# Two interleaved mixer and MLP layers on one core: finer groups at the hand-over to the first MLP, a new plan of priorities, and a store cut in halves

## The chip, the cores and the metric

The kernel runs on one core of one Trainium2 chip. The metric is device time in microseconds of one execution. The kernel before takes 249.48 us (median of 8 runs, 248.67 to 251.76).

A core has five engines that run their own instruction streams and meet at semaphores: TensorE (PE) multiplies matrices out of SBUF into PSUM; ScalarE (ACT) and VectorE (DVE) both can move PSUM to SBUF; GpSimd (POOL) does small things here; SyncE (SP) issues nearly all DMAs.

## The reference, cut to what matters

```
x = q                                            # (1, 2048, 512) bf16
x = x + layernorm(x) * y                         # mixer A
x = x + gelu(layernorm(layernorm(x)) @ w1 + b1) @ w2 + b2   # MLP B, F = 1376
x = x + layernorm(x) * y                         # A again, same y
x = x + gelu(layernorm(layernorm(x)) @ w1 + b1) @ w2 + b2   # B again
```

Here `y = irfft(rfft(kv) * rfft(ssm_k)) + kv * ssm_D`, and `kv` is the 4-tap causal filter of `k` with `shift_k`, times `v`. It doesn't depend on `x`, so it is computed once. The convolution along 2048 positions, 512 channels, is long; the kernel does it with matrix products in place of an FFT.

## The kernel before, in words

**Data.** The 2048 positions are 16 slices of 128 rows, 512 channels wide. Slice `s` holds positions `16 * p + s` on partition `p`. All SBUF lives in one big array `ar`, cut by hand into regions (`R_X` the running activation, `R_YT` the result `y`, `R_XT` and `R_HT` two buffers each for the transposed input and the hidden layer of the MLP); small floats are in `sm`, and PSUM is `ps`, eight banks.

**The mixer part** runs first and has these stages, each a run of matmuls into a PSUM tile of two banks, followed by an eviction to bf16 in SBUF by ACT or DVE (helper `evac`, L512: L515 is ACT's form, L516 DVE's):

- `ht` (L566 to 579): the filter `ssm_k`, loaded as 4 blocks of 128 channels, is transposed on PE (L573, 16 transposes per block).
- `h1` and `h2` (L608 to 615): two transform stages of the filter, PE lines L590 and L603. When all of `h2` is in `R_H`, 16 DMAs of 256 KB (L620; issued through the helper at L499) copy it to `R_HS` with the two halves of the partitions swapped.
- `fir0` to `fir3` (L623 to 672): the 4-tap filter of `k` for four groups of 128 channels. Groups 0 and 1 go through PE (L633 transposes, L645 products, L652 times `v`); groups 2 and 3 are eight DVE operations each in `shift_dve` (through the helper `tt`, L510). These form three products with taps into three shared temporaries, then add, multiply and add in turn.
- `x1_0` to `x1_3` (first transform of `kv`, L590), then for each half of the channels (`PARTS`: 64 groups of 4 channels each): `x2` (`products`: PE L691, an eviction, then a DVE product with both `R_H` and `R_HS`, L510), `i1` (first inverse stage, PE L715) and `i2` (second inverse stage, `inverse2`, PE L771). `inverse2` makes 4 slices of `y` at a time for one half of the channels: 8 matmuls of 256 columns and one eviction of 1024 columns.

**The MLP part** goes block by block over slices: in layer 0 in blocks of 2, 2, 2, 2, 4, 4 slices (`BLOCKS0`), in layer 1 of 4, 4, 4, 4. A block takes these steps: statistics on DVE (L799, L801) and the power -0.5 on POOL (L805, L807); the normalization on DVE (L814), times `y`, plus `x` (L510); statistics again; the second normalization; four 128 by 128 transposes per slice, on PE with an eviction for slices 0 to 3 of layer 0 (L858) and by DMA on SP's queue for the others (L850); `m1`, 11 groups of 4 matmuls, as wide as 128 times the block's slices (L871), each followed by a GELU on ACT (L876); `m2`, per slice 11 matmuls of 512 columns (L890) and one DVE addition to `x` (L894). In layer 1 finished slices are stored two at a time, 256 KB per DMA.

**The order of work** isn't written down by hand. Every operation is recorded with a cost in ns and its reads and writes; `Prog.schedule` then plays a list scheduler: the engine that can start earliest takes the ready operation of highest priority. The priority is the length of the path behind it plus a bias per stage from the table `BIAS`; `SHY` holds DVE back from evictions of a stage by so many ns; `LAT` is the assumed delay from one engine to another. What comes out is a fixed order for each engine and a choice of engine for every eviction; the costs have no other effect. DMAs keep their program order on SP's queue. `Pool` limits how many PSUM tiles of a kind may be open (four of two banks for the mixer part; two banks for transposes, three for `m1`, three for `m2`). The planner also emits the waits: an operation waits on its own engine too where it reads or overwrites what an earlier one there wrote or read (PE and SP excepted).

Of the kernel before, what the change touches and what calls it, by code (L numbers as in the profile page):

```python
# [44 lines left out]
class Prog:  # L45
# [5 lines left out]
    LAT = 130.0  # L51
    BIAS = {'fir0': 83800, 'fir1': -43400, 'fir2': 54600, 'fir3': -219300, 'h1': 39000, 'h2': 18300, 'ht': 155000, 'i1_0': -114900, 'i1_64': 24300, 'i2_0': -179500, 'i2_64': 54600, 'm1': 74700, 'm2': -45000, 'q0': 3500, 'q1': -4700, 'q2': 145200, 'q3': -6300, 'q5': -57000, 'q6': -80400, 'q7': -74600, 'x1_0': -53700, 'x1_1': 64300, 'x1_2': -7500, 'x1_3': 21300, 'x2_0': 210400, 'x2_64': 68700, 'z0': 9300, 'z1': -23300, 'z2': -64900, 'z3': 38400, 'z5': -30700, 'z6': -33300, 'z7': -12500}
    SHY = {'fir0': 1000, 'fir1': 0, 'h1': 150, 'h2': 0, 'ht': 3000, 'i1_0': 0, 'i1_64': 0, 'i2_0': 150, 'i2_64': 600, 'x1_0': 770, 'x1_1': 300, 'x1_2': 150, 'x1_3': 1000, 'x2_0': 600, 'x2_64': 0, 'z0': 600, 'z1': 600}
# [127 lines left out]
    def schedule(self):  # L181
# [29 lines left out]
        while done < n:  # L211
# [58 lines left out]
            for si in o.succ:  # L270
                q = ops[si]
                lat = self.LAT
                if not o.dma and len(q.engs) == 1 and q.engs[0] == o.eng:
                    lat = 0.0 if o.eng == PE or q.preds[o.i] == "psum" else 90.0
                q.ready = max(q.ready, o.end + lat)
                q.npred -= 1
                if q.npred == 0:
                    for x in q.engs:
                        ready[x].append(q)
# [147 lines left out]
AR = 105088  # L427
PE_CH = (0, 1)
LOADS = ("k", "v", 0, 1, 2, 3, 4, 5, 6, 7)
PARTS = ((0, 64), (64, 64))  # L430
BLOCKS0, BLOCKS1 = (2, 2, 2, 2, 4, 4), (4, 4, 4, 4)
NSPLIT = 4


def bass_interleave_layers__ssm_conv_h3__mixer_channel_mlp__prompt_kernel(
# [52 lines left out]
    R_SR, R_D = R_2, R_2 + 2048  # L488
    R_XT = R_S2
# [30 lines left out]
    E1 = {ACT: 1040.0, DVE: 1220.0}  # L520
# [40 lines left out]


# [4 lines left out]
    for b in range(4):  # L567
# [3 lines left out]
        def f(e, src=src, tl=tl):  # L571
            for a in range(16):
                r = e.transpose(QB(tl, 0, 128, a * 128, [1, 128]), src[a], IDN)  # L573
            return r
        P.op(PE, f, 16 * 80.0, reads=src + [IDN], tile=tl)
        evac(BOTH, A(0, 128, R_HP + b * 2048, [4, 16], [64, 32], [1, 4]),
             lambda tl=tl: QB(tl, 0, 128, 0, [128, 16], [4, 32], [1, 4]), {ACT: 1880.0, DVE: 1225.0}, tl)
# [18 lines left out]
    def stage2(G, ks, n):  # L596
# [8 lines left out]
        P.op(PE, f, len(ks) * 53.0, reads=[x for y in ins for x in y[1:]], tile=tl)  # L605
# [19 lines left out]
    def shift_pe(i):  # L625
# [5 lines left out]
        def f(e, src=src, tl=tl):  # L631
            for a in range(16):
                r = e.transpose(QB(tl, 0, 128, a * 128, [1, 128]), src[a], IDN)  # L633
            return r
        P.op(PE, f, 16 * 60.0, reads=src + [IDN], tile=tl)
        evac(BOTH, A(0, 128, R_KT[i] + 2, [130, 16], [1, 128]),
             lambda tl=tl: QB(tl, 0, 128, 0, [128, 16], [1, 128]), {ACT: 1880.0, DVE: 1225.0}, tl)
        for a8 in range(2):
# [8 lines left out]
            P.op(PE, f, 32 * 62.0, reads=[x for y in ins for x in y[2:]], tile=tl)  # L647
# [5 lines left out]
            P.op(DVE, g, 1200.0, reads=[v], writes=[o], tile=tl)  # L653

    def shift_dve(i):

        c = DV_CH[i]
        tm = [A(0, 128, R_TMP + 2048 * q, [128, 16], [1, 128]) for q in range(3)]

        def tap(j, o):  # L660
            tt(o, A(0, 128, R_K + (3 - j) * 512 + 128 * c, [512, 16], [1, 128]),
               A(0, 128, R_SJ + 512 * i + 128 * j, [0, 16], [1, 128]), ALU.mult, 1210.0,
               more=halo if j else ())
        for j in range(3):
            tap(3 - j, tm[j])
        tt(tm[1], tm[0], tm[1], ALU.add, 1210.0)
        tap(0, tm[0])
        tt(tm[2], tm[1], tm[2], ALU.add, 1210.0)
        tt(tm[1], tm[2], tm[0], ALU.add, 1210.0)
        tt(A(0, 128, R_KV + 2048 * c, [64, 32], [4, 16], [1, 4]),  # L670
           A(0, 128, R_TMP + 2048, [4, 32], [128, 16], [1, 4]),
           A(0, 128, R_V + 128 * c, [4, 32], [512, 16], [1, 4]), ALU.mult, 1220.0)
# [7 lines left out]
    def products(d0, n):  # L680
# [3 lines left out]
        for k0 in range(0, 128, nk):  # L684
# [4 lines left out]
            def f(e, ins=ins, tl=tl):  # L689
                for i, w, m in ins:  # L690
                    r = e.matmul(Q(tl, 0, 128, i * pitch, [1, n]), w, m, start=True, stop=True)  # L691
                return r
            P.op(PE, f, nk * 53.0, reads=[x for y in ins for x in y[1:]], tile=tl)
# [4 lines left out]
                 {ACT: 200 + .82 * w, DVE: 80 + 1.11 * w}, tl)  # L698
            x = A(0, 128, xo, [0, 2], [4 * nk, n // 4], [1, 4 * nk])
            h = A(0, 128, R_H + 128 * d0 + 4 * k0, [R_HS - R_H, 2], [512, n // 4], [1, 4 * nk])  # L700
            tt(h, x, h, ALU.mult, 80 + 1.11 * w)
# [19 lines left out]
    for c in range(4):  # L721
# [3 lines left out]
        else:  # L725
            shift_dve(DV_CH.index(c))
# [29 lines left out]
    def inverse2(d0, n):  # L756
# [3 lines left out]
        for a0 in range(0, 16, 2 * nb):  # L760
            tl = Tile(dconv)
            ins = []
            for al in range(2 * nb):
# [10 lines left out]
            t = 2 * nb * w  # L774
# [159 lines left out]
```

## Time and profile before

| what | value |
|---|---|
| time, median of 8 runs | 249.48 us |
| time of the profiled execution | 249.46 us |
| its span, first to last instruction | 247.7 us |
| mean granted TensorE clock | 0.992 |
| busy: PE, DVE, ACT, POOL | 227.5, 175.6, 136.4, 29.7 us |
| first matmul (transposes of `ssm_k`) | 5.05 us |
| first matmul of `inverse2` | 80.21 us |
| first matmul of the MLP | 89.75 us |
| last PE instruction of the span ends | 244.36 us |

How to read it: the span is 1.76 us shorter than the run's time, and this remainder lies outside what the engines' instructions show. A row of the groups gives the busy time and the mean duration of one instruction; back to back instructions overlap a little, so the pitch (the time of a run of them divided by their number) is shorter than this mean, above all on PE. In the timeline and in the chain, instructions of one line that follow each other are merged, with their count behind the x.

### The profile page before, as it was taken

What the parts mean: (1) busy time and instruction counts of PE and PEld (TensorE: products, weight loads), DVE (VectorE), ACT (ScalarE), POOL (GpSimd) and SP (SyncE); (2) the same over time, 40 slices, a digit from 0 to 9 for tenths busy, and PEclk for the clock granted to TensorE, in tenths of its full rate; (3) what the DMA queues carried; (4) which work ended last, traced back from release to release, by engine and by line L of the source; (5) the groups of instructions that cost most, each with busy time, mean ns of one, the idle gap of its engine ahead of it and who ended that gap; (6) DMA issues with size and microseconds to landing.
All of it is one profiled execution on the core that took longest, in us unless ns stands there. A gap on an engine that the chain in (4) does not pass through costs nothing.

```text
span 247.7 us, 5306 instructions
## 1 busy us (share of the span) xinstructions
PE 227.5 (92%) x2248; PEld 145.0 (59%) x2248; DVE 175.6 (71%) x358; ACT 136.4 (55%) x189; POOL 29.7 (12%) x58
## 2 busy tenths in 40 slices
PE   1988889787699979999999999999999999999994
PEld 1977779576699847775644444444444444444441
DVE  0798999989999888908999996378894732202233
ACT  2377798899998877753506517318228353072000
POOL 2320000000102042110111103005011010000000
PEclk9999999999999979999999999999999999999999
DMA  6999915999994000120130402200407123011112
GB/s 241 371 407 409 396 24 122 216 216 223 369 381 134 0 0 11 34 42 3 22 64 3 85 0 43 42 3 3 85 0 90 42 42 85 3 42 42 42 42 85
DMA packets 25480, 27.64 MB, mean 112 GB/s; under 512 B 17553, under 2 KB 19568, under 8 KB 25328
## 3 DMA queue, kind: packets, MB, share of 16 engines
q1 hardware_dynamic: 25310, 27.21, 37.9%
q8 instruction: 17, 0.28, 0.5%
q10 hardware_dynamic: 146, 0.10, 0.2%
q14 instruction: 7, 0.06, 0.1%
HBM read 17.34 MB, written 2.10 MB: 78 GB/s over the span
## 4 chain that ended last, share of the span: by engine, by line
PE 75%; ACT 7%; SPq 6%; DMA 5%; DVE 4%; issue 1%; DVEq 0%
PE ps L871 32%; PE ps L890 30%; SPq L499 6%; ACT ar L515 6%; PE ps L715 6%; DMA ar<-ar 3%; PE ps L590 2%; DVE ar L510 2%; PE ps L573 2%; DMA ar<-in_A_ssm_k_dram 2%; PE ps L645 2%; DVE ar L516 1%; DVE ar L894 1%; DVE ar L652 0%; ACT ar L537 0%
## 5 line engine op out<-in xcount | busy, mean ns | idle before, releaser
L876 ACT ACTIVATE ar<-ps,sm 128x512 bf16<-128x512 f32 (+3 forms) x110 | 63.5, 601 | 73.9 <-PE ps L871 52.9
L871 PE MATMUL ps<-ar 128*128 128x512 bf16 (+3 forms) x440 | 79.8, 342 | 1.1 <-ACT ar L515 1.1
L515 ACT ACTIVATE ar<-ps 128x1024 bf16<-128x1024 f32 (+2 forms) x76 | 70.7, 1038 | 16.0 <-PE ps L590 13.3
L890 PE MATMUL ps<-ar 128*128 128x512 bf16 (+1 forms) x352 | 78.1, 379 | 0.0
L871 PEld LDWEIGHTS ps<-ar 128*128 128x128 bf16 (+1 forms) x440 | 44.4, 102 | 35.5 <-ACT ar L515 1.2
L510 DVE TENSOR_TENSOR ar<-ar 128x512 bf16<-128x512 bf16 (+2 forms) x104 | 61.0, 643 | 0.9 <-ACT ar L515 0.7
L890 PEld LDWEIGHTS ps<-ar 128*128 128x128 bf16 (+1 forms) x352 | 34.3, 98 | 40.7
L894 DVE TENSOR_TENSOR ar<-ar,ps 128x512 bf16<-128x512 bf16 x32 | 21.1, 682 | 51.0 <-PE ps L890 51.0
L799 DVE BATCH_NORM_STATS2 sm<-ar 128x6 f32<-128x512 bf16 (+1 forms) x68 | 41.0, 646 | 0.0
L814 DVE TENSOR_SCALAR ar<-ar,sm 128x512 bf16<-128x512 bf16 x64 | 22.5, 405 | 7.2 <-POOL sm L807 5.4
L590 PE MATMUL ps<-ar 128*64 128x128 bf16 x512 | 17.8, 221 | 3.9 <-DVE ar L510 1.5
L516 DVE CAST ar<-ps 128x1024 bf16<-128x1024 f32 x17 | 20.1, 1219 | 1.1 <-PE ps L590 0.7
L807 POOL TENSOR_TENSOR sm<-sm 128x4 f32<-128x4 f32 (+1 forms) x20 | 18.6, 931 | 1.7
L590 PEld LDWEIGHTS ps<-ar 128*64 128x64 bf16 x512 | 14.9, 110 | 6.4 <-DVE ar L510 1.7
L805 POOL TENSOR_SCALAR sm<-sm 128x4 f32<-128x4 f32 (+1 forms) x20 | 4.3, 217 | 108.0 <-DVE sm L801 107.9
L715 PE MATMUL ps<-ar 128*128 128x128 bf16 x256 | 14.9, 220 | 1.7 <-DVE ar L510 1.4
L715 PEld LDWEIGHTS ps<-ar 128*128 128x128 bf16 x256 | 14.5, 114 | 1.9 <-DVE ar L510 1.5
L516 DVE COPY ar<-ps 128x2048 bf16<-128x2048 bf16 x5 | 6.1, 1226 | 8.0 <-PE ps L573 7.7
L691 PE MATMUL ps<-ar 128*128 128x64 bf16 x256 | 9.6, 194 | 2.0 <-ACT ar L515 1.5
L573 PE MATMUL ps<-ar 128*128 128x128 bf16 x64 | 5.8, 264 | 5.1 <-DMA ar<-in_A_ssm_k_dram 5.1
L691 PEld LDWEIGHTS ps<-ar 128*128 128x128 bf16 x256 | 8.2, 98 | 3.2 <-ACT ar L515 2.2
L603 PE MATMUL ps<-ar 128*128 128x128 bf16 x128 | 8.4, 220 | 1.8 <-ACT ar L515 0.9
(24 smaller groups left out, 70.7 us busy)
## 6 DMA issues: line engine op xcount, KB each, us to landing
ar<-tab_s SPq DMA_DIRECT2D x8, 512.0 KB, 16.2
ar<-ar SPq DMA_DIRECT2D x16, 256.0 KB, 6.6
ar<-in_A_ssm_k_dram SPq DMA_DIRECT2D x4, 512.0 KB, 5.5
ar<-in_A_k_dram SPq DMA_DIRECT2D x4, 512.0 KB, 9.5
ar<-in_A_v_dram SPq DMA_DIRECT2D x4, 512.0 KB, 13.5
ar<-in_A_q_dram SPq DMA_DIRECT2D x4, 512.0 KB, 12.7
out_dram<-ar SPq DMA_DIRECT2D x8, 256.0 KB, 2.0
ar<-in_B_w_dram SPq DMA_DIRECT2D x1, 1376.0 KB, 11.6
```

What stands on the lines that cost most here:

```text
L510: return P.op(eng, lambda e: e.tensor_tensor(o, a, b, op), dur, reads=[a, b] + list(more), writes=[o])
L515: return e.activation(dst, src(), AF.Copy)
L516: return e.tensor_copy(dst, src())
L590: r = e.matmul(Q(tl, 64 * ri, 64, i * 128, [1, 128]), w, m, start=True, stop=True)
L715: r = e.matmul(Q(tl, 0, 128, i * 128, [1, 128]), w, m, start=q == 0, stop=q == 1)
L799: P.op(DVE, lambda e, sj=sj, x=x: e.bn_stats(sj, x), 80.0 + 1.18 * w, reads=[x], writes=[sj], gate=gate)
L807: P.op(POOL, lambda e: e.tensor_tensor(r, v, hf, ALU.pow), 1020.0, reads=[v, hf], writes=[r])
L814: P.op(DVE, lambda e: e.tensor_scalar(o, x, m, r, ALU.subtract, ALU.mult), 405.0, reads=[x, m, r], writes=[o])
L871: r = e.matmul(Q(tl, 0, rows, 0, [1, w]), a, m, start=dk == 0, stop=dk == 3)
L876: P.op(ACT, lambda e, dst=dst, tl=tl, rows=rows, bias=bias, w=w: e.activation(dst, Q(tl, 0, rows, 0, [1, w]), AF.Gelu_apprx_tanh, bias=bia ...
L890: r = e.matmul(Q(tl, 0, 128, 0, [1, 512]), ins[fc][0], ins[fc][1], start=fc == 0, stop=fc == 10)
L894: P.op(DVE, lambda e, x=x, tl=tl: e.tensor_tensor(x, x, Q(tl, 0, 128, 0, [1, 512]), ALU.add), 690.0, reads=[x], writes=[x], tile=tl)
```

## The change

- **Second inverse stage.** `inverse2` makes slices 0 and 1, then 2 and 3, then 4 to 7, 8 to 11 and 12 to 15: ten tiles in place of eight; the first two of each half have 4 matmuls and an eviction of 512 columns.
- **Blocks.** Layer 0 goes in blocks of 1, 1, 2, 2, 2, 2, 2, 2, 2 slices; layer 1 stays. The temporaries of the normalization rotate over eight places in place of six.
- **Zero matmuls ahead of h.** POOL zeroes 512 columns (`R_W`) at the start, and PE multiplies them by themselves 8 times, 512 columns wide, into a PSUM tile that nobody reads. A like facility ahead of the MLP is there with a count of zero (`NWARM`).
- **Last slice.** In layer 1, `m2` of slice 15 is made in two halves of 256 columns, each with its own addition and its own store of 64 KB; slice 14 is stored alone.
- **Shift on DVE.** The order of the taps and the places change: one accumulator per channel group, and a temporary in the place where the group's `kv` will go, so that the two groups share no buffer; eight DVE operations per group as before. (`PO_CH`, empty, would put groups on POOL.)
- **Plan.** New values of `BIAS`, `SHY`, `LAT` (130 to 155 ns; from one operation to the next on the same engine 90 to 50) and of most recorded costs, and finer stage names in the MLP (one for each block: `q` statistics and normalization, `y` products, `z` second statistics). Of the biases, `h2` goes from 18300 to 147100, `ht` from 155000 to 209900, `h1` from 39000 to 4900, `fir0` from 83800 to 47900, `x2_0` from 210400 to 149200, `x2_64` from 68700 to 106500, `i2_0` from -179500 to -83000, `i2_64` from 54600 to -41700.

```diff
...
-    LAT = 130.0
...
+    LAT = 155.0
...
-                    lat = 0.0 if o.eng == PE or q.preds[o.i] == "psum" else 90.0
+                    lat = 0.0 if o.eng == PE or q.preds[o.i] == "psum" else 50.0
...
-BLOCKS0, BLOCKS1 = (2, 2, 2, 2, 4, 4), (4, 4, 4, 4)
+BLOCKS0, BLOCKS1 = (1,1,2,2,2,2,2,2,2), (4, 4, 4, 4)
 NSPLIT = 4
+NWARM = 0
...
+    R_W = place(512)
...
-    E1 = {ACT: 1040.0, DVE: 1220.0}
+    E1 = {ACT: 950.0, DVE: 1160.0}
...
+    def warm(pool, n, w, dur, gate=()):
+
+        tl = Tile(pool)
+        z = A(0, 128, R_W, [1, w])
+
+        def f(e):
+            for i in range(n):
+                r = e.matmul(Q(tl, 0, 128, 0, [1, w]), z[:, :128], z, start=True, stop=True)
+            return r
+        P.op(PE, f, n * dur, reads=[z], tile=tl, prio=-1e9, gate=gate)
+
+    z = A(0, 128, R_W, [1, 512])
+    P.op(POOL, lambda e, z=z: e.memset(z, 0.0), 400.0, writes=[z], prio=1e6)
+    P.tag = "warm0"
+    warm(dconv, 8, 512, 427.0)
...
-    def shift_dve(i):
+    def shift_tt(i):
 
         c = DV_CH[i]
-        tm = [A(0, 128, R_TMP + 2048 * q, [128, 16], [1, 128]) for q in range(3)]
+        eng, d = (POOL, 4080.0) if c in PO_CH else (DVE, 1140.0)
+        acc, tmp = [A(0, 128, o, [128, 16], [1, 128]) for o in (R_TMP + 2048 * i, R_KV + 2048 * c)]
...
-        for j in range(3):
-            tap(3 - j, tm[j])
-        tt(tm[1], tm[0], tm[1], ALU.add, 1210.0)
-        tap(0, tm[0])
-        tt(tm[2], tm[1], tm[2], ALU.add, 1210.0)
-        tt(tm[1], tm[2], tm[0], ALU.add, 1210.0)
+        tap(0, acc)
+        for j in range(1, 4):
+            tap(j, tmp)
+            tt(acc, acc, tmp, ALU.add, d, eng)
...
-        for a0 in range(0, 16, 2 * nb):
+        for a0, na in ((0, nb), (nb, nb), (2 * nb, 2 * nb), (4 * nb, 2 * nb), (6 * nb, 2 * nb)):
             tl = Tile(dconv)
             ins = []
-            for al in range(2 * nb):
+            for al in range(na):
...
-        return R_N + (nn[0] % 6) * 512
+        return R_N + (nn[0] % 8) * 512
...
+                if L and s == 15:
+                    for c in range(0, 512, 256):
+                        tc = tl if not c else Tile(pm2)
+
+                        def f(e, ins=ins, tc=tc, c=c):
+                            for fc in range(11):
+                                r = e.matmul(Q(tc, 0, 128, 0, [1, 256]), ins[fc][0], ins[fc][1][:, c:c + 256], start=fc == 0, stop=fc == 10)
+                            return r
+                        P.op(PE, f, 11 * 109.0, reads=[x for y in ins for x in y], tile=tc)
+                        x = A(0, 128, R_X + s * 512 + c, [1, 256])
+                        P.op(DVE, lambda e, x=x, tc=tc: e.tensor_tensor(x, x, Q(tc, 0, 128, 0, [1, 256]), ALU.add), 400.0,
+                             reads=[x], writes=[x], tile=tc)
+                        outs.append(dma(dr(out, 512 * s + c, [16 * 512, 128], [1, 256]), x, 1 << 16, reads=[x], writes=[]))
+                    continue
...
-            if L == 1:
-                for c in range(0, n, 2):
...
+                if L and (s % 2 or s == 14):
+                    q = 1 if s == 14 else 2
+                    src = A(0, 128, R_X + (s + 1 - q) * 512, [1, 512 * q])
+                    outs.append(dma(dr(out, 512 * (s + 1 - q), [16 * 512, 128], [1, 512 * q]), src, q << 17, reads=[src], writes=[]))
...
```

## The prediction

> **What bounds the kernel now.** I read the page's slices first, then the chain that ended last in order of time, then busy times by stretches cut where the chain changes engine, then the timeline of two places.
>
> The page's engine shares and its 40 slices of 6.2 us each:
>
> ```profile
> PE 227.5 (92%) x2248; PEld 145.0 (59%) x2248; DVE 175.6 (71%) x358; ACT 136.4 (55%) x189; POOL 29.7 (12%) x58
> ...
> PE   1988889787699979999999999999999999999994
> ...
> DVE  0798999989999888908999996378894732202233
> ACT  2377798899998877753506517318228353072000
> ...
> PEclk9999999999999979999999999999999999999999
> ```
>
> The reader should see two kernels in one. From slice 15 on (about 90 us) PE is full; before it DVE is full, ACT nearly so, and PE has holes. The clock row has one dip, at slice 15. The chain in order of time (start us, us, what):
>
> ```profile
> 5.05 4.54 PE ps L573 x48
> ...
> 54.78 8.30 DMA ar<-ar
> ...
> 81.28 8.43 ACT ar L515 x10
> ...
> 89.75 6.64 PE ps L871 x44
> ...
> 98.57 4.80 PE ps L871 x44
> ...
> 243.74 1.34 DVE ar L894 x2
> ```
>
> Five places matter: the first transposes; the swap copies, which land at 63.08 just when DVE takes their result; ten evictions in a row on ACT, after which the MLP can start; the first 44 matmuls of the MLP, which take 6.64 us where the next like group takes 4.80; and the tail on DVE. The stretches (from:to, length, busy us of each engine with its instructions, granted clock, DMA):
>
> ```profile
> 10.00:17.20 7.20, 6.05 (x171) 5.39 (x167) 6.61 (x6) 5.81 (x7) 3.39 (x5) 1.00 1.02 388
> 17.20:38.50 21.30, 18.50 (x355) 16.20 (x349) 19.85 (x18) 17.83 (x19) 0.38 (x2) 1.00 0.71 267
> 38.50:63.10 24.60, 19.32 (x496) 16.79 (x496) 23.80 (x21) 22.39 (x25) 0.52 (x1) 1.00 0.97 211
> 63.10:67.50 4.40, 3.56 (x81) 3.33 (x82) 4.40 (x5) 4.17 (x6) 0.23 (x1) 1.00 1.04 387
> ...
> 87.40:89.75 2.35, 0.72 (x8) 0.45 (x8) 2.27 (x9) 2.30 (x4) 0.15 (x2) 1.00 0.00 0
> ...
> 98.40:243.70 145.30, 145.30 (x739) 72.67 (x738) 88.53 (x234) 58.52 (x99) 16.61 (x27) 1.00 0.18 39
> ```
>
> The last row has PE busy for all of its 145.3 us at full clock: nothing can be won there by order. What can be won lies before 98.4 us and in the tail. From 10 to 67.5 us DVE is idle for only 0.59 + 1.45 + 0.80 + 0 = 2.84 us, ACT for 1.39 + 3.47 + 2.21 + 0.23 = 7.30 us. They share the evictions, so that stretch could shrink by at most about (2.84 + 7.30) / 2 = 5.1 us, with not a hole left.
>
> **Zero matmuls ahead of h.** Today PE waits to 5.05 us for `ssm_k`; 48 transposes then take 4.54 us (95 ns each), the last 16 take 1.22 us (76 each), and later, at full speed, L715 does 224 matmuls of the same width in 12.89 us (57.5 each):
>
> ```profile
> 67.48 12.89 PE L715 MATMUL ps<-ar 128*128 128x128 bf16 x224 [0.28 <-ACT ar L515]
> ```
>
> So the first transposes run near half speed, though the profile's clock says 1.00 there. DVE's four evictions behind them start at 7.01, 8.48, 9.7 and 11.35 us, with holes of 0.24 and 0.49 between. The change adds one memset on POOL (nearest rows 0.52 to 0.73 us for a memset on one partition; POOL starts at 0.72, and what is pushed back there isn't wanted before 8.3 us) and 8 matmuls of 512. At twice the 216 ns that these take at full speed (9.50 us / 44) that is 3.46 us: from about 1.3 to 4.8 us, ahead of the data, so it costs nothing; were the memset slower by a microsecond, it would push the transposes 0.7 us. With a warm clock a block's transposes take 1.0 in place of 1.7 us: the first eviction starts at 6.1 in place of 7.01, and the four end at about 11.0 in place of 12.58, a gain of 0.9 to 1.6 us on DVE. [...] Range 0 to -1.5; I take -1.0.
>
> **New plan, stages up to the last product.** No instruction is added here; the order and the choice of engine change. The costs written into the planner are nearer to the trace: an eviction of 1024 columns on ACT goes from 1040 to 950 ns, and the trace has 15 in 14.52 us (968); DVE's from 1220 to 1160, and the trace has two in 2.34 us (1170). A plan by truer costs should leave fewer holes. `h2` gains 129 us of priority: its last eviction ends at 38.53 us and the 16 copies wait for it on SP's queue, with all loads of `q`, `w1` and `w2` behind them. The last table piece is issued at 16.91 us and takes some 16 us, so h2 can't be done before about 34 to 35 us: the copies may go up to 3.5 us earlier. DVE, though, is full, and only holes can be saved. Best case -5.1 + the share that the warm clock already takes, say -4; worst case a plan with holes doubled, +5. I take a fifth of the holes' 5.1: -1.0.
>
> **Shift on DVE.** Eight operations per group, as before, but each now needs the one before it: if the two chains aren't interleaved, the pitch is the full mean of 1.222 us, where overlapping ones run at 8.03 / 7 = 1.147; 16 times 0.075 = +1.2 at most. The two groups no longer share a buffer, and other work fits between. I take +0.2.
>
> **Second inverse stage and the first blocks.** PE starts `inverse2` at 80.37, and the MLP begins at 89.75. In between lie 7.1 us of `inverse2` and 0.72 us of transposes, so 1.7 us of holes; then the clock drops:
>
> ```profile
> 90.00:91.00 1.00, 1.00 (x7) 0.70 (x5) 1.00 (x4) 0.30 (x1) 0.63 (x1) 0.50 0.00 0
> ```
>
> It is at 0.50 to about 93.3 us, and costs 6.64 - 4.80 = 1.84 us. [...] So at most 1.7 + 1.8 = 3.5 us are to be had. The new path to the first MLP matmul: 4 matmuls 0.44, two evictions of 512 (0.53 each, from 0.97 less half its 1024 columns) 1.06, product and sum of the last half 0.46, its statistics 0.42 and 0.20, POOL with gaps 1.2 (L807 takes 1075 ns for four values and 715 for two, so 0.54 for one), normalization and hops 0.5, transposes 0.4, eviction and hops 0.65: 5.3 us, so 85.7. But the start isn't the price. ACT then owes work:
>
> ```profile
> L876 ACT ACTIVATE ar<-ps,sm 128x512 bf16<-128x512 f32 x60 | 40.3, 687 | 61.9 <-PE ps L871 45.4 <-PE ps L890 16.4
> ...
> L876 ACT ACTIVATE ar<-ps,sm 128x256 bf16<-128x256 f32 x40 | 17.7, 473 | 11.3 <-PE ps L871 6.7 <-PE ps L890 4.5
> ```
>
> A GELU of 128 columns is then about 473 - 107 = 366 ns, or 0.33 in a run (those of 256 run at 3.65 / 8 = 0.456, with PE's pace in it): 3.65 us for one slice, where PE's 44 matmuls take 44 x 57.5 ns = 2.53 us. ACT's evictions of `inverse2` take 4 x 0.53 + 6 x 0.95 = 7.8 us, two slices' transposes 1.1, two slices' GELUs 7.3: with 81.0 as its start, 97.2. PE could have done by then 7.1 + 1.2 + 5.1 + 2.4 = 15.8 us of work, so up to 96.2. ACT holds PE for about 1 us in place of 3.5, and 5.06 for two blocks of one replace 4.80: -2.5 + 0.3, and some 0.3 for the order in which evictions and GELUs take turns: -1.9. Bounds: -3.2 if DVE takes some evictions; +1.5 if PE waits for GELUs at each small block and the clock stays low. [...]
>
> **Blocks of two in place of four.** Twice 4 slices at 9.50 us become 2 x 4.80 to 4.82: +0.25 in all. More and smaller statistics on POOL lie under full PE. SP's transposes stay 28. Each block has only 9.6 us of PE for the next one's preparation, and DVE needs about 4.0 us per slice: it is idle most of 105 to 115 us, so this is covered; without the cover, PE would wait.
>
> **Tail.** PE ends at 244.36; an addition of 0.67, an issue of 0.33, a landing 2.0 us after the issue, and the end of the span at 247.7. Half an addition is about 0.41 (682 ns less 256 of the 1.05 ns per column between 512 and 1024), so -0.27; 64 KB in place of 256 saves between nothing and 192 KB at the 400 GB/s of the loads, 0.48. The other half's store has 1.2 us of matmuls to hide under. 22 matmuls of 256 at 109 ns take what 11 of 512 took. I take -0.5.
>
> Sum: -1.0 - 1.0 + 0.2 - 1.9 + 0.25 - 0.5 = -3.95, rounded to -3.9. From the profiled execution: span 247.7 - 3.9 = 243.8, plus the 1.76 us around it, 245.6. That execution's 249.46 is the median but for 0.02, so **245.6 us**.
>
> **The rivals.** *ACT takes PE's place at the hand-over* (chance 0.2). The one-slice blocks are ACT's: 3.65 against 2.53 us. If GELUs queue behind evictions, PE stands 1 us per block and after each for the last GELU, and the clock falls again, so that only warm-up and tail count: -1.5, 248.0. For it: ACT is full from 81.28 to 89.71 already. Against: it is idle for 2.7 of the 8.65 us that follow. *The plan packs the first stretch* (0.12): -3 there in place of -1, 243.4. For it: 7.3 us of ACT holes and copies that could start 3.5 us sooner; against: DVE, 95% busy, must give up work to ACT. *The swap copies become the bound* (0.18), slower: they run from 38.56 to 63.08 and DVE takes the last just as it lands, so there is no slack. Each microsecond that the last eviction of `h2` is planned later moves the products, `i1` and all behind them by one. Past 3.9 + 1.3 us later, at 43.7, the kernel is slower; at 45 it is 252. Against: the bias of `h2` goes up; but that of `h1`, which feeds it, goes down by 34 us, and a new order there can hold it. *The zero matmuls don't open the clock* is in the bounds of their item: 246.6.
>
> **How the numbers follow.** The forecast has 0.5, and its own range is 244.0 to 247.5. Range of all: 242.8 takes in most of the packed case, 250.4 the ACT case and the nearest of the slow one; about 0.15 of slow cases and 0.04 of fast ones lie outside. Half a percent (1.25 us) is about what a measurement of this kernel can tell from no change. Faster: 0.49 of the forecast, 0.12 of the ACT case, all 0.12 of the packed one: 0.73. Same: 0.01, 0.08 and 0.01 of the slow case, 0.10. Slower: 0.17.
>
> **What would show it.** L573 at 60 to 65 ns from its first block, its first eviction near 6.1; DVE idle less than 2.8 us between 10 us and the last product, which today ends at 72.5; `h2` done near 35 to 37; the first L871 near 85 to 87 with the clock at 1.00 behind it; PE full from about 95 on; last PE to end of span 2.8 us in place of 3.3. The forecast is wrong if L871's first groups show waits on ACT of over 2 us in sum, if the clock drops to 0.5 again, if the copies land after 63, or if PE shows holes at blocks of two.

## The result, and the profile after

The changed kernel takes 247.65 us (median of 19 runs, 246.97 to 248.42), the kernel before 249.46 (56 runs, 247.85 to 252.43): 1.8 us less. The ratio on record is 0.9919, interval 0.9898 to 0.994; the two medians alone give 0.9927. The forecast was 245.6 with a range of 242.8 to 250.4: the right way, and about half the size (1.8 us by the medians, 2.0 by the ratio, where 3.9 were forecast). Not only the median moved: the runs of after lie within 1.5 us, those of before within 4.6.

The profiled execution of after took 248.08 us and has a span of 246.3, 1.4 less than before's. Its page, the busy shares and slices:

```profile
PE 229.3 (93%) x2399; PEld 154.5 (63%) x2399; DVE 175.3 (71%) x361; ACT 140.8 (57%) x222; POOL 34.1 (14%) x71
...
PE   7978789896699999999999999999999999999994
...
DVE  0759999999798898889999967999587203002233
ACT  2297898999799897674454443633266130772000
```

There are 151 more matmuls and 33 more ACT instructions. The row of the clock is gone from the page, since nothing moved in it: the dip at slice 15 isn't there. PE has holes up to slice 11 (about 68 us), as before it. The chain in order of time:

```profile
5.67 11.92 DMA ar<-in_A_k_dram
...
56.06 8.40 DMA ar<-ar
...
64.48 9.18 DVE ar L513 x8
...
89.91 2.41 PE ps L897 x40
...
98.03 4.80 PE ps L897 x44
...
242.54 0.67 PE ps L930 x3
...
243.23 0.69 DVE ar L934
```

The chain no longer starts with the transposes: DVE waits for `k`. The swap copies land at 64.46 and DVE takes them after a wait, where it came just in time before. And what ends last isn't a half of slice 15 but a full addition (L934) of slice 14. The stretches, cut at the same events:

```profile
10.00:17.60 7.60, 5.84 (x167) 4.94 (x164) 4.08 (x4) 6.85 (x9) 3.19 (x4) 1.00 1.03 390
17.60:39.67 22.07, 19.04 (x352) 17.10 (x352) 22.06 (x20) 18.79 (x19) 1.42 (x2) 1.00 0.70 257
39.67:64.46 24.79, 20.16 (x529) 17.50 (x527) 22.89 (x20) 23.17 (x25) 0.52 (x1) 1.00 0.96 205
...
88.70:89.90 1.20, 0.62 (x8) 0.45 (x8) 1.20 (x7) 1.09 (x2) 0.00 (x0) 1.00 0.00 0
...
98.03:243.20 145.17, 145.16 (x836) 81.98 (x833) 92.09 (x244) 61.12 (x121) 19.97 (x38) 1.00 0.17 39
```

DVE is idle for 7.60 - 4.08 = 3.5 us before `k` lands (0.6 before), and for 1.9 us while the copies run (0.8 before); in between it is full. From 98 us on PE is full, as before.

Marks of the two profiled executions, us from the start:

| mark | before | after | after less before |
|---|---|---|---|
| last swap copy lands | 63.08 | 64.46 | +1.4 |
| last DVE product ends | 72.5 | 73.66 | +1.2 |
| first matmul of `inverse2` | 80.21 | 81.54 | +1.3 |
| first MLP matmul | 89.75 | 89.91 | +0.2 |
| `m1` of slices 2 and 3 starts | 98.57, 8 of `m2` done | 98.03, 12 done | -0.5 - 4 x 0.216 = -1.4 |
| PE's end | 244.36 | 243.19 | -1.2 |
| span | 247.7 | 246.3 | -1.4 |

So the first stretch lost 1.3 us, the hand-over won 2.7, the blocks of two gave back about 0.2 and the tail won 0.2. That is one execution of each; the runs below show that it isn't the whole story.

### The profile page after: what moved, and what is told of

Read it like the earlier page. It is cut to its first block, busy times and chain, and to the rows that moved or that the text cites. A ratio compares the mean times of both kernels' runs of the same rounds, so it can differ in the third digit from the quotient of the medians.

```text
span 246.3 us, 5660 instructions
## 1 busy us (share of the span) xinstructions
PE 229.3 (93%) x2399; PEld 154.5 (63%) x2399; DVE 175.3 (71%) x361; ACT 140.8 (57%) x222; POOL 34.1 (14%) x71
## 4 chain that ended last, share of the span: by engine, by line
PE 64%; DVE 12%; DMA 8%; SPq 8%; ACT 2%; issue 2%; POOL 1%
PE ps L897 31%; PE ps L930 30%; SPq L502 8%; DVE ar L513 8%; DMA ar<-in_A_k_dram 5%; DMA ar<-ar 3%; DVE ar L519 2%; ACT ar L518 2%; PE ps L734 1%; PE ps L919 1%; POOL sm L830 1%; DVE sm L822 1%; PE ps L790 1%; DVE ar L672 1%; PE ps L623 0%
## 5 line engine op out<-in xcount | busy, mean ns | idle before, releaser
L902 ACT ACTIVATE ar<-ps,sm 128x256 bf16<-128x256 f32 (+5 forms) x143 | 67.1, 523 | 69.5 <-PE ps L930 55.1
L897 PE MATMUL ps<-ar 128*128 128x256 bf16 (+4 forms) x572 | 80.0, 297 | 0.5 <-DVE ar L519 0.5
L518 ACT ACTIVATE ar<-ps 128x1024 bf16<-128x1024 f32 (+1 forms) x76 | 71.4, 1041 | 7.0 <-PE ps L610 2.9
L897 PEld LDWEIGHTS ps<-ar 128*128 128x128 bf16 (+1 forms) x572 | 53.2, 100 | 26.8 <-DVE ar L519 0.7
L930 PEld LDWEIGHTS ps<-ar 128*128 128x128 bf16 (+1 forms) x341 | 33.2, 98 | 37.5
L934 DVE TENSOR_TENSOR ar<-ar,ps 128x512 bf16<-128x512 bf16 x31 | 20.7, 682 | 44.7 <-PE ps L930 44.7
L830 POOL TENSOR_TENSOR sm<-sm 128x2 f32<-128x2 f32 (+2 forms) x26 | 20.2, 777 | 2.2
L610 PE MATMUL ps<-ar 128*64 128x128 bf16 x512 | 17.8, 221 | 2.8 <-ACT ar L518 1.9
L519 DVE CAST ar<-ps 128x1024 bf16<-128x1024 f32 (+1 forms) x16 | 18.0, 1154 | 3.2 <-PE ps L610 1.7
L734 PE MATMUL ps<-ar 128*128 128x128 bf16 x256 | 15.3, 220 | 3.5 <-DVE ar L513 1.6
L828 POOL TENSOR_SCALAR sm<-sm 128x2 f32<-128x2 f32 (+2 forms) x26 | 5.6, 216 | 92.2 <-DVE sm L824 92.0
L519 DVE COPY ar<-ps 128x2048 bf16<-128x2048 bf16 (+1 forms) x8 | 7.2, 923 | 6.8 <-PE ps L593 6.8
L824 DVE BATCH_NORM_AGGREGATE sm<-sm 128x2 f32<-128x6 f32 (+1 forms) x64 | 10.3, 174 | 0.2
L623 PE MATMUL ps<-ar 128*128 128x128 bf16 x128 | 8.4, 220 | 1.5 <-ACT ar L518 1.0
```

What stands on the lines that cost most here:

```text
L518: return e.activation(dst, src(), AF.Copy)
L519: return e.tensor_copy(dst, src())
L610: r = e.matmul(Q(tl, 64 * ri, 64, i * 128, [1, 128]), w, m, start=True, stop=True)
L734: r = e.matmul(Q(tl, 0, 128, i * 128, [1, 128]), w, m, start=q == 0, stop=q == 1)
L830: P.op(POOL, lambda e: e.tensor_tensor(r, v, hf, ALU.pow), 430.0 + 150.0 * n, reads=[v, hf], writes=[r])
L897: r = e.matmul(Q(tl, 0, rows, 0, [1, w]), a, m, start=dk == 0, stop=dk == 3)
```

## The experiments

**The clock in every run.** Each run comes with its span and its mean granted TensorE clock, and these fall into three groups. In before's profiled execution the drop lasts 3.41 us (0.50 from 89.93 to 93.34). At half clock for 3.4 us out of 247, the mean falls by 0.5 x 3.4 / 247 = 0.007; so 0.993 is one drop and 0.986 two. The table has the 79 runs of before that came with the experiments, and the 20 of after, the profiled one among them:

| kernel | no drop (0.997 and up): runs, median us | one drop | two drops |
|---|---|---|---|
| before | 8, 248.33 | 40, 249.34 | 31, 250.86 |
| after | 12, 247.58 | 8, 247.75 | none |

A mean of 0.997 to 0.999 counts as no drop: in the two profiled executions of this kind the half clock comes only after PE's last matmul. Most of before's spread is the number of drops, at 1.0 to 1.5 us each; its runs without one still lie between 247.53 and 248.99. In after's runs a drop costs 0.2, and none has two. Without drops the two kernels differ by 0.75 us only; the other microsecond of the 1.8 is drops. This made the questions: which part closes the drops, and where the rest went.

**Zero matmuls in the kernel before.** The memset and the 8 matmuls at the head of POOL and PE, nothing else moved:

```diff
+                    if e == POOL:
+                        eng.memset(self.zero, 0.0).then_inc(zs, 1)
+                    if e == PE:
+                        eng.wait_ge(zs, 1)
+                        for i in range(8):
+                            eng.matmul(self.bank7, self.zero[:, :128], self.zero, start=True, stop=True)
```

> The kernel before, its order on every engine unchanged, with the memset and the 8 zero matmuls put at the head of POOL and PE. Theory W (the prediction's item): the first transposes run at 60 to 65 ns, DVE's fourth eviction ends 0.9 to 1.6 us sooner and most of it reaches the end: about 1.0 us faster, ratio 0.996. Theory K (what the trace of after suggests): what is won is lost at the next load, DVE then waits for the first piece of k, which lands at 17.2 to 17.6 us; time within 0.3 us of before. With either, DVE's first eviction starts at 6.1 to 6.7 us.

Measured 248.31 us (12 runs), before 249.71 beside it: ratio 0.9944, 0.9915 to 0.9974. Its timeline on DVE (start, length, engine, line, count, in brackets the wait):

```profile
6.04 3.83 DVE L524 COPY ar<-ps 128x2048 bf16<-128x2048 bf16 x3 [6.04 <-PE ps L581]
10.35 1.23 DVE L524 COPY ar<-ps 128x2048 bf16<-128x2048 bf16 x1 [0.48 <-PE ps L581]
11.49 4.61 DVE L524 CAST ar<-ps 128x1024 bf16<-128x1024 f32 x4
17.76 1.23 DVE L518 TENSOR_TENSOR ar<-ar 128x2048 bf16<-128x2048 bf16 x1 [1.66 <-DMA ar<-in_A_k_dram]
```

The evictions start at 6.04 and the fourth ends 1.0 us sooner, as theory W has it; then DVE stands 1.66 us for `k`, where it stood 0.16, as theory K has it. The time sides with W: -1.4 us. This profiled execution has a drop from 17.8 us on (behind PE's hole of 1.29 us while `k` is awaited), which took back what its trace could have shown. At the same number of drops its runs are about 1.0 us faster: two without a drop are at 247.2 and 247.4, nine with one at 248.38. One run of 12 has two drops, against 31 of 79. Where the microsecond is kept past the wait for `k` isn't settled: ACT is 0.5 us busier from 10 to 17.5 us than in before (6.46 against 5.98), so some evictions of `h1` came sooner.

**One of the zero matmuls in the kernel after**, with the same order:

```diff
-            for i in range(n):
+            for i in range(1):
                 r = e.matmul(Q(tl, 0, 128, 0, [1, w]), z[:, :128], z, start=True, stop=True)
```

> The kernel after with the same order on every engine, but only one of the 8 zero matmuls is executed. Theory W: the first transposes fall back to 95 ns and the kernel loses 0.7 to 1.3 us. Theory K: DVE waits for k until 17.6 us either way, and the time stays within 0.3 us of after.

247.38 us (8 runs), after 247.65: theory K. DVE's fourth eviction ends at 12.45 us in place of 11.64, and its wait for `k` is 2.05 us in place of 1.82. In the order of after, the zero matmuls are worth nothing that 8 runs can show.

**Filled holes at the hand-over of the kernel before**, order unchanged: matmuls into a free bank, overwritten later.

```diff
+    P.fill = {z0[0]: 2, m1[0]: 4}
```

> The kernel before, its order unchanged, with 2 matmuls of 512 columns put before PE's first transposes of the MLP and 4 before its first m1, into a bank that is free there; their result is overwritten. Nothing else is done sooner. Theory C (the clock's dip is a cost of its own): granted clock 1.00 from 89 to 94 us, the first m1 block takes 4.8 us in place of 6.64, and the time falls by 1.5 to 1.8 us, ratio about 0.993. Theory E (the dip lies in time that PE would have waited anyway, for its GELUs): under 0.4 us. If the two fillers delay their followers, up to 0.3 us is lost against that.

249.43 us (12 runs), ratio 0.9985, 0.9944 to 1.0025: no gain that can be told in the median. But six of the twelve runs have no drop, at 247.91, against 8 of 79; two have one (40 of 79 before), four have two (250.82), about the same share as before. This puts the one drop of most runs of before at the hand-over. The profiled execution has two, and they lie elsewhere (from:to, length, busy of PE, PEld, DVE, ACT, POOL, then the granted clock):

```profile
49.00:51.00 2.00, 0.64 (x16) 0.48 (x16) 1.97 (x2) 2.00 (x4) 0.00 (x0) 1.00 0.99 203
51.00:54.40 3.40, 3.10 (x62) 2.93 (x63) 1.97 (x3) 2.79 (x3) 0.00 (x0) 0.60 1.04 213
...
61.00:64.60 3.60, 2.32 (x62) 1.85 (x58) 3.60 (x5) 3.48 (x4) 0.38 (x1) 1.00 0.95 302
64.60:68.00 3.40, 2.18 (x21) 2.18 (x22) 3.40 (x5) 2.29 (x3) 0.14 (x1) 0.61 1.03 393
```

Each drop follows a hole of PE: 1.5 us near 49 and 1.4 us near 62. The second one hits the first tiles of the inverse stage, which stand on the critical chain.

The traces show more of what stands ahead of a drop. Thirteen of the profiled executions have changes of the clock on record. In each of them these lie whole multiples of 3.413 us apart (before's own are at 8.01, 89.93 and 93.34 us: 24 times that, and once), and a drop before PE's end lasts just one of these. Cut at such distances from its drops, this execution has the following stretches:

```profile
48.25:51.67 3.42, 1.63 (x46) 1.31 (x48) 3.35 (x4) 3.42 (x4) 0.00 (x0) 1.00 1.04 220
51.67:55.08 3.41, 3.41 (x68) 3.24 (x63) 1.94 (x2) 2.42 (x4) 0.00 (x0) 0.50 1.03 203
...
61.91:65.32 3.41, 1.69 (x46) 1.33 (x42) 3.41 (x4) 3.23 (x4) 0.52 (x1) 1.00 0.98 349
65.32:68.73 3.41, 2.91 (x28) 2.91 (x29) 3.41 (x4) 2.37 (x4) 0.00 (x0) 0.50 1.04 382
```

Ahead of each drop stands a stretch in which PE is busy for about half the time, 1.63 of 3.42 us and 1.69 of 3.41. Before's own profiled execution has the same two holes, at 48.64 to 50.15 and 62.05 to 63.45. Its changes of the clock lie elsewhere; cut at the same distances from them, the emptiest stretches over these holes have PE busy for 2.18 and 2.01 us of 3.41, and there is no drop behind them. Its one drop follows the stretch at the hand-over, with 1.73:

```profile
48.97:52.38 3.41, 2.18 (x66) 1.93 (x67) 2.67 (x3) 3.28 (x4) 0.00 (x0) 1.00 1.02 216
59.21:62.62 3.41, 2.01 (x52) 1.57 (x48) 3.41 (x4) 3.39 (x5) 0.50 (x1) 1.00 1.03 259
...
86.52:89.93 3.41, 1.73 (x18) 1.12 (x17) 3.33 (x12) 3.18 (x5) 1.05 (x3) 1.00 0.00 0
```

Over these thirteen traces, the eleven such stretches ahead of a drop inside the kernel have PE busy for 35 to 51%. One with 48% has no drop behind it; in before's own trace all others up to PE's end have 59% or more. So the drops on record come behind sparse stretches, but no share that sets one off is shown. Where the changes of the clock fall against the program differs from one execution to the next, by up to 2.7 us in these traces (there is one at 51.67 in this execution; before's own distances give 52.38); that this is why the same program drops in one and not in another is an estimate of the author's from these figures. The two drops above start 13.65 us apart, four times 3.413, and the two holes 13.4, which may be why two drops come together. The first of the crossed kernels below has its two drops, in its profiled execution, at the same times as this one (51.68 and 65.33).

**All three holes of the kernel before filled:**

```diff
+    fill(s1, 5, s1, s2)
+    fill(i1, 4, i1, s2)
+    fill(z0[0], 2, m1[2], t2)
+    fill(m1[0], 4, m1[2], t2)
```

> The kernel before, its order unchanged, with filler matmuls of 512 columns in three of PE's holes: 5 before the ninth tile of the last long row of L590 (hole of 1.5 us at 48.6), 4 before the first tile of L715 (hole of 1.4 us at 62.1), and 2 and 4 at the hand-over as in x2. [...] Theory O (the drops fall where PE waits anyway): median within 0.4 us of before.

248.36 us (12 runs), ratio 0.994, 0.9911 to 0.9969. None of the twelve runs has a drop (the lowest mean clock is 0.997), though they still lie between 247.66 and 249.22. Theory O had the median within 0.4 us of before; it is 1.3 below the 249.67 beside it. The same stretches, now at full clock:

```profile
49.00:51.00 2.00, 1.71 (x23) 0.70 (x19) 1.97 (x3) 2.00 (x3) 0.00 (x0) 1.00 0.98 221
51.00:54.40 3.40, 3.06 (x94) 2.69 (x95) 2.67 (x3) 3.24 (x4) 0.00 (x0) 1.00 1.04 208
...
61.00:64.60 3.60, 2.71 (x43) 1.75 (x44) 3.60 (x4) 3.47 (x5) 0.52 (x1) 1.00 0.94 311
64.60:68.00 3.40, 3.26 (x77) 2.95 (x74) 3.40 (x4) 3.28 (x4) 0.00 (x0) 1.00 1.05 388
```

Matmuls whose results nobody uses win 1.3 us, with the order of all others unchanged: the drops are a cost of their own.

**The two halves of the change crossed.** The part up to the last tile of the first inverse stage (engines and order) from one kernel, the rest from the other. First before's part with after's rest (groups, blocks, tail), and with after's zero matmuls and shift on DVE:

```diff
+                if o.cid in where and self.FORCE[e][nextc[e]] != o.cid:
+                    continue
```

> The kernel after (zero matmuls, small groups, small blocks, tail), but with the engines and the order of the kernel before for everything up to the last tile of the first inverse stage. If after's plan is what put the last product at 73.0 to 73.7 us in place of 72.5, this one has it at 71.7 to 72.7 and is 0.5 to 1.2 us faster than after: 246.5 to 247.1. If the swap copies and the load of k, and not the plan, set it, within 0.3 us of after. If the clock's drops come with before's plan of that stretch, runs at 0.986 appear, and it is not faster than after.

248.62 us (12 runs), ratio 0.9938, 0.9908 to 0.9967: 1.0 slower than after, and drops are back, as the third of these cases has it. Without drops 247.75 (5 runs), with one 248.83 (6), with two 249.91 (1). Then after's part, and its shift on DVE, with before's rest:

> The kernel before (hand-over with groups of four, blocks of 2 and 4, tail, no zero matmuls), but with the engines and the order of the kernel after, and its shift on DVE, up to the last tile of the first inverse stage. If the gain of after over before comes from the hand-over, this is at before, or up to 1.2 us slower: 249.5 to 250.7. If it comes from a first stretch with fewer drops of the clock, the runs at 0.986 vanish and the median is 248.5 to 249.2, though the last product is no sooner.

248.90 us (11 runs; a twelfth, of 1316 us, is left aside), ratio 0.999, 0.9966 to 1.0013: no gain that can be told from none. But no run has two drops. Nine have none, at 248.85; two have one, at 248.92.

The two halves are not crossed cleanly, since the first of these kernels has the zero matmuls and the second has not, and both have the new shift. Beside the runs above they read:

| kernel | median us (without drops) |
|---|---|
| before | 249.71 (248.33) |
| before with the zero matmuls | 248.31 (247.3, two runs) |
| first part in before's order, zero matmuls, new shift; rest of after | 248.62 (247.75) |
| first part of after without zero matmuls; rest of before | 248.90 (248.85) |
| after with one zero matmul | 247.38 (247.42) |
| after | 247.65 (247.58) |

Down the one way, the zero matmuls win 1.4, after's rest with the new shift then nothing (+0.3), and after's order 1.0. Down the other, after's first part wins 0.8, after's rest 1.5, and the zero matmuls nothing (+0.3). So the gain doesn't split into parts with a worth of their own. After's rest with before's order and the old shift was not run, so what that rest is worth there without the shift is open. The medians come from several sets of runs, in which before lies at 249.46 to 250.20, so a few tenths say nothing.

The profiles tell two things more. From the first `inverse2` matmul to the end of the span it is 165.7 to 165.8 us in the four profiled executions that have before's rest and no drop there, and 167.45 in before's own, with its drop at the hand-over. With after's rest as it stands it is 164.75 to 164.9 (four executions). So after's rest is worth 1.0 us at full clock, and 2.7 only against an execution with that drop. And the new shift costs time where its operations follow one another, since each needs the one before it. In before's order, first with the old shift (the kernel before with the zero matmuls), then with the new one:

```profile
20.84 3.49 DVE L518 TENSOR_TENSOR ar<-ar 128x2048 bf16<-128x2048 bf16 x3
38.84 4.62 DVE L518 TENSOR_TENSOR ar<-ar 128x2048 bf16<-128x2048 bf16 x4
```

```profile
19.81 3.73 DVE L536 TENSOR_TENSOR ar<-ar 128x2048 bf16<-128x2048 bf16 x3
38.90 4.91 DVE L536 TENSOR_TENSOR ar<-ar 128x2048 bf16<-128x2048 bf16 x4
```

The four runs of such operations take 15.4 us with the old shift and 16.2 with the new: +0.8. In after's own order, where the two groups take turns at first, the same reading gives about +0.5.

**Half of the swap copies in the kernel after**: each copy moves half its columns and POOL zeroes the others, so half of the products with swapped parts are left out.

```diff
-                dma(dst, src, 1 << 18, reads=[src], rate=210.0)
+                dh, sh = [A(64 * p, 64, r + 128 * d0 + c, [1, 1024]) for p, r in ((1 - g, R_HS), (g, R_H))]
```

> The kernel after with the same order, but each of the 16 swap copies moves only half of its columns (the other half of each place is zeroed by POOL between 15 and 30 us, so the products there are left out in effect). Theory S (the copies bound the stretch): DVE doesn't wait 1.2 to 1.7 us for them at 62.8 us, the last product ends at 71.8 to 72.3 in place of 73.0 to 73.7, and the time falls by 1.2 to 1.7 us, 246.0 to 246.5. Rival: DVE's or ACT's work takes its place, under 0.5 us.

247.04 us (6 runs), 0.6 less than after. DVE, first after, then this one:

```profile
53.58 9.17 DVE L513 TENSOR_TENSOR ar<-ar 128x2048 bf16<-128x2048 bf16 x8
64.48 9.18 DVE L513 TENSOR_TENSOR ar<-ar 128x2048 bf16<-128x2048 bf16 x8 [1.73 <-DMA ar<-ar]
```

```profile
53.48 18.35 DVE L513 TENSOR_TENSOR ar<-ar 128x2048 bf16<-128x2048 bf16 x16
```

The wait is gone and the last product ends at 71.8: theory S for the stretch. Only two runs had no drop, at 246.1 and 246.2, which is the full 1.4 under after's runs without a drop; the other four are at 247.25, with a drop, in the profiled one at 62.9 us, where this order now starts the inverse stage. So the median misses the range that theory S set, and a stall removed can be eaten by the clock.

**Parts of the hand-over in the kernel after**, its first part held:

```diff
-        for a0, na in ((0, nb), (nb, nb), (2 * nb, 2 * nb), (4 * nb, 2 * nb), (6 * nb, 2 * nb)):
+        for a0, na in ((0, 2 * nb), (2 * nb, 2 * nb), (4 * nb, 2 * nb), (6 * nb, 2 * nb)):
```

> The kernel after, with its own order up to the last tile of the first inverse stage, but the second inverse stage in groups of 4 slices as before; blocks of 1, 1, 2, ... stay. If the small groups are what lets the MLP start sooner after them (8.4 us from the first L790 to the first m1 in place of 9.5), this needs 8.9 to 9.4 us and is 0.4 to 1.0 us slower than after. Rival: ACT and POOL set the start, not the groups, and it is within 0.3 us of after.

```diff
-BLOCKS0, BLOCKS1 = (1,1,2,2,2,2,2,2,2), (4, 4, 4, 4)
+BLOCKS0, BLOCKS1 = (2,2,2,2,2,2,2,2), (4, 4, 4, 4)
```

> The kernel after, with its own order up to the last tile of the first inverse stage and its small groups, but layer 0 in eight blocks of 2 slices. Against it the blocks of one save POOL's second column (0.18 us twice) and one slice's statistics and normalization ahead of the first m1. If they matter, the first m1 comes 1.0 to 1.5 us later and the time is 0.5 to 1.2 us longer than after, less the 0.26 us that two blocks of one take more on PE. Rival: within 0.3 us of after.

251.62 and 250.27 us (12 runs each), ratios to before 1.0038 (1.0011 to 1.0065) and 1.0012 (0.9985 to 1.004): against after's median 4.0 and 2.6 us slower, more than either theory had. But not where they had it. From the first `inverse2` matmul to the first `m1` it is 8.2 us (80.46 to 88.69) and 8.3 us (81.83 to 90.09), where after has 8.4 and before 9.5. They lose later, PE on the coarse groups' kernel:

```profile
148.95 4.98 PE L921 MATMUL ps<-ar 128*128 128x256 bf16 x44 [1.71 <-DMA ar<-ar]
```

PE waits for a transpose by DMA; from 140 to 180 us it is idle for 2.9 us there, and for 2.4 us in the kernel with blocks of two, where after has no hole. The table of priorities was made for other stages and blocks, which is likely why the planner let a transpose come late. So the first `m1` comes as soon after `inverse2` with either of the two undone. No run has both undone with after's priorities, so whether one of them is enough, or whether the order around them does it, isn't shown; nor is what they are worth with an order that suits them.

**Slice 14 ahead of the halves:**

```diff
-                P.tag = "m2"
+                P.tag = "m2_14" if L and s == 14 else "m2"
```

> The kernel after, but slice 14's last three matmuls, its addition and its 128 KB store come ahead of slice 15's halves, so that a half is what ends last. If the tail is what the halves were to cut, the stretch from PE's end to the span's end goes from 3.1 to 2.7 us, and the time falls by 0.3 to 0.5 us. Rival: the length of the store doesn't matter, and only the shorter addition shows: 0.2 us or less.

PE's end to the span's end is 245.2 - 242.7 = 2.5 us, after has 3.1. The median is 247.65 (8 runs, 246.56 to 248.38), that of after. A gain of 0.6 in the trace can't be seen in so few runs with such a spread; it isn't shown in time.

**Planned anew.** In after's own plan the loads of `k` end at 15.9 us and the trace has 17.6; the copies take 22.4 us there and 24.8 in the trace. With these two figures mended, slice 14 ahead, and new `BIAS` and `SHY` from a random search on the plan's length:

```diff
-                o.end = dma_free + 1900.0
+                o.end = dma_free + 1900.0 + self.LATE.get(o.i, 0.0)
...
-                dma(dst, src, 1 << 18, reads=[src], rate=210.0)
+                dma(dst, src, 1 << 18, reads=[src], rate=193.0)
```

> The kernel after with slice 14 ahead of the halves, and planned anew with two figures of its planner put nearer to the trace: the loads of k land 1.7 us later (17.6 us in the trace, 15.9 in the plan) and the swap copies move 193 bytes per ns in place of 210; new BIAS and SHY by a search with that plan's own length. It ends h2 some 2 us sooner in the plan. If the planner's early k is why after's first stretch came out late, the copies land at 62 to 63 us in place of 64.5, the last product ends at 71.5 to 72.7, and the time is 246.0 to 247.0. If the clock's drops or DVE's own work decide, it is within 0.4 us of after, or slower.

> As the other replanned kernel, from another start of the search: h2 ends as in after's plan, the first m1 comes soonest in the plan. If the end of h2 is what counts, it lies between after and the other one, 246.5 to 247.4; if the hand-over counts, it is the faster of the two, 246.0 to 246.8.

246.42 and 244.54 us (6 runs each), ratios to before 0.985 (0.9809 to 0.9891) and 0.9777 (0.9736 to 0.9818). The first lies in its own range; the second lies below both of its ranges, so neither theory had its size. It beats both kernels: before by 2.2%, and after's median, taken in another set of runs, by about 3 us. Its DVE before `k` and at the products, and PE at the hand-over:

```profile
14.94 1.22 DVE L520 CAST ar<-ps 128x1024 bf16<-128x1024 f32 x1 [0.60 <-PE ps L611]
17.17 1.23 DVE L520 CAST ar<-ps 128x1024 bf16<-128x1024 f32 x1 [1.01 <-PE ps L611]
18.31 2.35 DVE L514 TENSOR_TENSOR ar<-ar 128x2048 bf16<-128x2048 bf16 x2
...
52.82 18.25 DVE L514 TENSOR_TENSOR ar<-ar 128x2048 bf16<-128x2048 bf16 x16 [0.40 <-ACT ar L519]
```

```profile
78.89 6.30 PE L791 MATMUL ps<-ar 128*128 128x256 bf16 x56
85.03 0.39 PE L885 MATMUL ps<-ar 128*128 128x128 bf16 x4
85.25 1.04 PE L791 MATMUL ps<-ar 128*128 128x256 bf16 x8
86.12 1.30 PE L898 MATMUL ps<-ar 128*128 128x128 bf16 x20
```

DVE does evictions of `h1` where it stood for `k`, the copies start at 37.64 in place of 39.67, the products run without a gap and end at 71.07, and the first `m1` follows `inverse2` in 7.2 us, with PE still at it when the first slice is transposed. Both new plans have the mended figures and end up 1.9 us apart, and the one with the earlier end of `h2` (copies from 36.62) is the slower: so the end of `h2` isn't what decides, and how much of the gain comes from the mended figures and how much from the search isn't separated. The planner didn't see the difference: by its own clock the two are 244.4 and 244.3 us long, after is 245.0 and before 251.6.

## Why the prediction was right or wrong

The direction held, and the measured time lies in the range. The size, and most of the steps behind it, did not.

- **What bounds the kernel**: right for the MLP. For the first stretch it took DVE's and ACT's work as the limit and counted their holes; the loads of `k` at 17.6 us and the copies at 64.5 are limits too, and the clock is a third. DVE's holes from 10 us to the last product were to fall below 2.8 us; they grew to 5.5.
- **Zero matmuls, -1.0**: failed for this change. The clock does change sooner with them: in eight profiled executions with all eight matmuls its first change on record is at 4.0 to 7.3 us, in the five with one or none at 8.0 to 10.7 (after's has no change on record); the first 32 transposes of after take 2.57 us, 80 ns each, where before's first 48 take 95 each. The step that failed is that four earlier evictions carry to the end; in after's order DVE waits for `k` (1.8 us with them, 2.05 without), and one matmul does as well as eight. In before's order they were worth 1.4, or 1.0 at the same number of drops, as the step had it. No run before the forecast shows the 0 at the end of this term's range, which was the author's estimate; in after's order about 0 is what the runs showed. The first eviction came at 6.67, not 6.1, in the profiled execution, at 6.06 in another of the same first part.
- **New plan, -1.0**: failed. The last product came 1.2 us later in the profile, and at full clock the new first part with before's rest is 0.5 slower (248.85 against 248.33). `h2` did not end at 35 to 37 but at 39.65, so the copies landed at 64.46, past the 63 that was named as a sign of being wrong. The rival "the swap copies become the bound" happened, but with `h2` 1.1 us later, where 5.2 were reckoned to turn the sign. What the order did win, about 1.0 beside after's rest, goes with fewer drops.
- **Shift on DVE, +0.2**: +0.8 in DVE's time in before's order, about +0.5 in after's, inside the +1.2 that was its bound. What of it reaches the end isn't shown: in after, DVE waits 1.7 us for the copies behind it.
- **Hand-over, -1.9**: right in kind: -2.7 by the marks, with 0.6 us of holes in place of 1.7 and no drop. But 1.7 of this is the drop of one execution; hand-over, blocks and tail together win 1.0 at full clock, where their three terms make -2.15. The step took the drop of one execution for a cost of every run; most likely half of the runs have it (the 40 of 79 with one drop). And the reason given, small groups and blocks of one, isn't shown to be what shortens the path; with either undone it stays at 8.2 to 8.3 us. The first `m1` was set for 85.7 by a chain of rows and came at 89.91, 8.4 us after the first `inverse2` matmul where 5.3 were reckoned: the chain assumed an ACT and DVE free for slice 0 alone, and they did slice 1's work and other evictions in between. The 57.5 ns for matmuls of 128 columns nearly held: 40 in 2.41 us, 60 ns each.
- **Blocks of two, +0.25**: about +0.2 by the marks.
- **Tail, -0.5**: -0.2. The halves don't end last; the planner put slice 14's last matmuls behind them. The step took the order of the text for the order of the work; with slice 14 put first, PE's end to the span's end is 0.8 us shorter than before.
- **What it didn't have at all**: drops of the clock other than the one in the profile shown. That one execution had one drop; 31 of 79 runs have two, at holes near 49 and 62 us in the executions that were profiled, which the prediction left out. A microsecond of the measured gain is theirs.

The sum of -3.9 thus had two terms of -1.0 that weren't there in after's order, and the gain measured has one of about -1.0 that wasn't in the sum. That the measured time came as near to the forecast as it did is in part luck.

## What to carry to other kernels

When the times of a kernel spread over 2% while its order of work is fixed, sort the runs by granted clock first: drops may be most of the spread. Filling PE's holes with matmuls that nobody reads won 1.3 us here, most of what the whole change did. Before an item of work at the start is made faster, look for the next thing that its consumer waits for; a gain ahead of a load that lands no sooner for it can be lost there, as it was in after's order (DVE took `k` at 17.61 us with eight zero matmuls, at 17.60 with one), though not in before's. A plan made by a cost model is as good as its landing times: compare a few of them with the trace before tuning priorities on it.

## What the runs showed that was not expected

- Holes of PE of 1.5 and 1.4 us were followed by 3.4 us at half clock each in one execution (from 51.67 and 65.32 us, before with its hand-over filled), and by none in another with the same order up to there (before's own); of 79 runs of before 8 had none, 40 one and 31 two, 1.0 to 1.5 us apart. In the 3.41 us ahead of each of the eleven drops inside the kernel that the traces have, PE was busy for 35 to 51%; in before's own execution PE was busy for 64 and 59% of the emptiest 3.41 us over the two holes.
- The profile's clock reads 1.00 from the start, though the first transposes ran at 95 ns in place of 57.5. The trace's clock records begin with the first change, at 8.01 us in the profiled execution of before; what lies ahead of it isn't recorded, and counts as full.
- 8 zero matmuls of 512 columns took 3.6 us (3.2 in another execution) from 1.30 us on, and ended before `ssm_k` landed: they did not delay it.
